# Moving one weight load ahead of a query load, and casts between VectorE and GpSimd, at the start of a fused attention and MLP kernel

## The chip, the cores and the metric

The kernel runs on one core of a Trainium2 chip. The metric is the time of one execution in microseconds (us) of device time. It is about 1.8 us longer than the span that the profile shows (first to last instruction). Engines are called as in the profile: PE is the matmul engine (TensorE), DVE is VectorE, ACT is ScalarE, POOL is GpSimd, SP issues DMAs. All timed runs of this study were in the fast state; the granted clock was 0.993 to 1.0 in all of them but three, which are named below. A load has landed when its data are in place.

## The reference, cut to what matters

```python
q_s = softmax(q, axis=-1)                    # q, k, v: (8 batches, 8 heads, 576, 64) f32
k_s = softmax(k, axis=2)                     # over the sequence
kv  = einsum('bhsd,bhse->bhde', k_s, v)      # 64 x 64 per head
x   = einsum('bhsd,bhde->bhse', q_s, kv)     # then laid out as (4608, 512)
h   = x @ w_in                               # 512 x 2048
g   = h * sigmoid(beta * h)
out = g @ w_out                              # 2048 x 512, f32
```

Inputs and outputs are float32; the kernel computes in bf16.

## The kernel before

Work runs in nine chunks of 512 rows of x (one per batch, and one for the leftover rows). For a chunk `c`, `mm_a(c, j)` computes one of 16 blocks of h (4 matmuls, then a tanh on ACT and a product on DVE, which gives `g`), and `mm_b(c, j)` adds `g` times a block of `w_out` into four accumulators (4 matmuls). In this text h_12 is `mm_a(0, 12)` of the first chunk, th_12 its tanh, g_12 its product. There are two PSUM buffers for h, so h_12 cannot start before tanh and product of h_10 are done.

While PE works on chunk 0, the weights still come in, and the attention of batch 1 is made ready: exp of q (ACT), row sum, reciprocal and multiply (DVE), transposes `tp` of q (PE) with an evacuation each (the copy out of PSUM, the memory that PE writes to), exp of k (ACT), cast of v to bf16, then `kv_mm` and `x_mm`.

```python
    load_q(0, parts=2); load_kv(k_st, k, 0, ...); load_kv(v_st, v, 0, ...)   # written in one line here
    ...
    w_load("in", 2)
    w_load("out", 2)
    load_q(1, parts=2)
    w_load("in", 3)                  # last block of w_in
    w_load("out", 3, 0)
    load_kv(k_st, k, 1, "k_st", parts=4)
    w_load("out", 3, 1)
    load_kv(v_st, v, 1, "v_st", parts=2)
    ...
    for kind, blk in (("in", 0), ("out", 0)):       # casts of the first weight blocks
        for half in range(2):
            if (kind, half) != ("in", 0):
                w_cast(kind, blk, half, nc.gpsimd)
    ...
    w_cast("in", 1, 0, nc.vector)
    mm_a(0, 2)
    mm_a(0, 3)
    w_cast("in", 1, 1, nc.vector)
    mm_b(0, 0)
    mm_b(0, 1)
    ...
    tail_zero(0)                                     # four memsets on POOL
    pool_cast(("out", 1), ("in", 2), ("out", 2))     # casts on POOL
    tail_zero(1)
    pool_cast(("in", 3), ("out", 3))

    for u in range(4, NJ):
        ...                                          # mm_a(0, u)
        if FIX and u in (12, 14):
            for j in (u - 12, u - 11):
                q_pet(1, j, nc.scalar if u == 12 else nc.vector)   # transposes
        mm_b(0, u - LAG)                             # LAG = 2
        if u in (9, 10):
            q_exp(1, u - 9)
        if u in (9, 11):
            q_sum(1, (u - 9) // 2)
        if u in (10, 12):
            q_mul(1, (u - 10) // 2)
        ...
        if u >= 12:
            kz_exp(1, u - 12)
        if u == 14:
            vz_cast(1, 0, nc.vector, m=2)
    mm_b(0, NJ - 2)
    vz_cast(1, 2, nc.vector, m=2)
    kv_mm(1, 0)
    kv_norm(1, 0)
    warm(2)                                          # two filler matmuls
    kv_mm(1, 1)
    kv_norm(1, 1)
    mm_b(0, NJ - 1)
    for j in range(HP):
        x_mm(1, j, ...)                              # first one: x_0 of batch 1
```

Each engine executes its instructions in the order of the program.

The softmax here doesn't subtract the row's maximum and nothing guards it: scores larger than these inputs give would overflow.

## Time and profile before

| | before |
|---|---|
| time, median of the first 3 runs | 290.23 us (290.08 to 290.25) |
| the profiled execution | 290.86 us, span 289.1 us |
| PE busy | 97% of the span, granted clock 1.0 |
| PE waits named after 51 us | only 0.2 us, in the last block |

From the page: the span, the busy times, and the slices of PE, its clock and the DMA engines.

```profile
span 289.1 us, 4130 instructions
...
PE 279.2 (97%) x1595; PEld 127.9 (44%) x1595; DVE 181.9 (63%) x281; ACT 163.7 (57%) x238; POOL 41.0 (14%) x55
...
PE   8899979999999999999999999999999999999994
...
PEclk9999999999999999999999999999999999999999
DMA  7999999907951982198129902794370033005003
```

PE is nearly always busy. One slice is 7.2 us; the DMA engines are full in slices 2 to 8, up to about 55 us, with the weights and the first batches. From there on PE sets the pace. The waits of PE say where the rest is:

```profile
PE h_12_520 L358 <- POOL w_in_b L145: 1.5, 1, 1.5
PE warm_153 L450 <- DVE kvp L478: 1.2, 1, 1.2
PE tp_0_200 L250 <- ACT ek_144 L158: 1.0, 1, 1.0
PE h_6_433 L358 <- DVE g_4_414 L370: 0.5, 1, 0.5
```

The second and third lie in the first 9 us and the change does not touch them. The PE timeline (columns: start, duration, engine, line, what, and in brackets the idle time before it and who ended it) gives the waits more exactly. A 512-column matmul starts 0.216 us after the one before it when nothing is in the way (the beat below), although its modelled duration is longer.

```profile
21.69 0.38 PE L386 MATMUL acc_3_380<-w_out_b,g_1_355 128*128 128x512 bf16 x1
22.16 1.04 PE L358 MATMUL h_4_407<-xT_80,w_in_b 128*128 128x512 bf16 x4
...
25.40 0.38 PE L386 MATMUL acc_3_380<-w_out_b,g_3_374 128*128 128x512 bf16 x1
26.30 1.02 PE L358 MATMUL h_6_433<-xT_80,w_in_b 128*128 128x512 bf16 x4 [0.51 <-DVE g_4_414 L370]
...
36.44 0.38 PE L386 MATMUL acc_3_380<-w_out_b,g_9_479 128*128 128x512 bf16 x1
38.34 0.60 PE L358 MATMUL h_12_520<-xT_80,w_in_b 128*128 128x512 bf16 x2 [1.52 <-POOL w_in_b L145]
...
49.95 0.38 PE L314 MATMUL x_0_666<-qsT_529,kvp 128*128 128x512 bf16 x1
```

Subtracting the beat: 0.25 us before h_4, 0.68 before h_6, 1.68 before h_12. The last line, x_0 of batch 1, is the mark by which I measure all versions below.

What held h_6 is on DVE and POOL. First DVE, then POOL:

```profile
21.40 0.69 DVE L145 CAST w_in_b<-w_in_102 128x1024 bf16<-128x1024 f32 x1 [0.96 <-DMA w_in_102<-in_moe_w_in_dram]
...
23.21 2.45 DVE L145 CAST w_in_b<-w_in_102 128x1024 bf16<-128x1024 f32 x1
25.57 0.67 DVE L370 SCALAR_TENSOR_TENSOR g_4_414<-th_4_412,h_4_407 128x512 bf16<-128x512 bf16 x1
```

```profile
22.63 1.04 POOL L145 CAST w_out_b<-w_out_100 128x1024 bf16<-128x1024 f32 x1 [4.53 <-DMA w_out_100<-in_moe_w_out_dram]
23.61 0.96 POOL L558 MEMSET vt_75<- 128x1040 bf16 x1
24.51 0.53 POOL L559 MEMSET ekt_77<- 128x512 bf16 x1
24.98 0.75 POOL L561 MEMSET vt_75<- 64x8 bf16 x2
...
36.65 2.62 POOL L145 CAST w_in_b<-w_in_114 128x1024 bf16<-128x1024 f32 x2 [2.11 <-DMA w_in_114<-in_moe_w_in_dram]
```

Two DVE casts of one shape took 0.69 and 2.45 us; the slow one ran beside POOL instructions. The Trainium skill, "SBUF — State Buffer", section "Who interferes with whom", explains it: DVE in a two-port mode and POOL take turns on a port pair, and the later one waits. The last POOL line is what held h_12: POOL had been idle for 2.11 us until the load of the last w_in block landed.

### The profile page before, as it was taken

Reading aid. Unit: us, or ns where it says so; the run is one execution under the profiler, and the core shown is the slowest. Engines: PE = TensorE matmul, PEld = TensorE weight load, DVE = VectorE, ACT = ScalarE, POOL = GpSimd, SP = SyncE. Lnnn points to the kernel's source line nnn. Section 1 sums busy time; section 2 is a strip of 40 time slices with the busy share of each in tenths; the row PEclk is TensorE's granted clock in tenths of the full one; section 3 lists DMA queues with packets and bytes.
Section 4 is the critical chain, followed back from the end, with each engine's and each line's share of the span. In section 5 each row is a group of like instructions: output and inputs, shape, how many; then the busy total and the mean of one; then the engine's idle time right before and its main releaser. Section 6 shows DMA issues by size and latency. Waiting matters only on the chain.

```text
span 289.1 us, 4130 instructions
## 1 busy us (share of the span) xinstructions
PE 279.2 (97%) x1595; PEld 127.9 (44%) x1595; DVE 181.9 (63%) x281; ACT 163.7 (57%) x238; POOL 41.0 (14%) x55
## 2 busy tenths in 40 slices
PE   8899979999999999999999999999999999999994
PEld 3443435444444444444444444444445444444441
DVE  7838577696569546945695469546954595454442
ACT  4762666694477356734683568355934563553341
POOL 4438660210030011000300030003000000000000
PEclk9999999999999999999999999999999999999999
DMA  7999999907951982198129902794370033005003
GB/s 228 383 384 364 379 389 315 285 2 183 322 168 40 309 218 95 50 322 225 64 84 234 313 29 120 171 259 116 145 213 7 1 147 73 0 0 147 0 0 145
DMA packets 56227, 50.08 MB, mean 173 GB/s; under 512 B 26240, under 2 KB 47760, under 8 KB 56208
## 3 DMA queue, kind: packets, MB, share of 16 engines
q1 hardware_dynamic: 56064, 49.56, 55.6%
q8 instruction: 12, 0.20, 0.3%
q10 hardware_dynamic: 144, 0.26, 0.2%
q14 instruction: 7, 0.06, 0.1%
HBM read 36.71 MB, written 9.44 MB: 160 GB/s over the span
## 4 chain that ended last, share of the span: by engine, by line
PE 83%; DMA 6%; DVE 5%; ACT 2%; SPq 1%; issue 1%; ACTq 0%
DMA w_in_102<-in_moe_w_in_dram 4%; DMA v_st_91<-in_v_dram 2%; PE acc_3_2822 L386 1%; PE acc_3_1636 L386 1%; PE acc_1_1026 L386 1%; PE acc_1_2820 L386 1%; PE acc_3_2577 L386 1%; PE acc_0_2248 L386 1%; PE acc_3_1940 L386 1%; PE acc_1_1938 L386 1%; PE acc_0_721 L386 1%; PE acc_1_2575 L386 1%; PE acc_0_2574 L386 1%; PE acc_2_2250 L386 1%; PE acc_1_1634 L386 1%; PE acc_3_1332 L386 1%
## 5 line engine op out<-in xcount | busy, mean ns | idle before, releaser
L358 PEld LDWEIGHTS <-w_in_b 128*128 128x128 bf16 x576 | 55.2, 98 | 70.5 <-issue 3.2
L145 POOL CAST va_2284<-v_st_2104 128x2048 bf16<-128x2048 f32 x1 | 1.9, 1919 | 30.7 <-DMA v_st_2104<-in_v_dram 30.7
L450 PEld LDWEIGHTS <-kvp 128*128 128x128 bf16 x34 | 3.6, 113 | 5.9 <-issue 3.1
L145 POOL CAST va_1669<-v_st_1489 128x2048 bf16<-128x2048 f32 x1 | 1.9, 1918 | 28.2 <-DMA v_st_1489<-in_v_dram 28.2
L145 POOL CAST va_1973<-v_st_1793 128x2048 bf16<-128x2048 f32 x1 | 1.9, 1916 | 25.9 <-DMA v_st_1793<-in_v_dram 25.9
L158 ACT ACTIVATE ek_144<-k_st_86 64x576 bf16<-64x576 f32 x8 | 5.4, 681 | 0.2
L158 ACT ACTIVATE ek_149<-k_st_118 64x576 bf16<-64x576 f32 x8 | 5.4, 677 | 0.0
L145 POOL CAST va_1061<-v_st_836 128x2048 bf16<-128x2048 f32 x1 | 1.9, 1918 | 24.2 <-DMA v_st_836<-in_v_dram 24.2
L314 PEld LDWEIGHTS <-kvp 128*128 128x128 bf16 x32 | 3.1, 98 | 4.3 <-DVE kvp L309 1.0
L145 POOL CAST va_1365<-v_st_1185 128x2048 bf16<-128x2048 f32 x1 | 1.9, 1919 | 21.4 <-DMA v_st_1185<-in_v_dram 21.4
L145 POOL CAST va_147<-v_st_91 128x576 bf16<-128x576 f32 x4 | 3.1, 805 | 6.5 <-DMA v_st_91<-in_v_dram 6.5
L214 ACT ACTIVATE eq_189<-q_st_83 128x1024 bf16<-128x1024 f32 x2 | 2.1, 1057 | 3.0 <-DMA q_st_83<-in_q_dram 3.0
L145 DVE CAST w_in_b<-w_in_102 128x1024 bf16<-128x1024 f32 x2 | 3.1, 1570 | 1.0 <-DMA w_in_102<-in_moe_w_in_dram 1.0
L145 POOL CAST va_783<-v_st_132 128x2048 bf16<-128x2048 f32 x1 | 1.9, 1919 | 12.4 <-DMA v_st_132<-in_v_dram 12.4
L145 POOL CAST w_in_b<-w_in_114 128x1024 bf16<-128x1024 f32 x2 | 2.6, 1334 | 2.1 <-DMA w_in_114<-in_moe_w_in_dram 2.1
L145 POOL CAST w_out_b<-w_out_100 128x1024 bf16<-128x1024 f32 x2 | 2.1, 1040 | 4.8 <-DMA w_out_100<-in_moe_w_out_dram 4.8
L225 DVE TENSOR_REDUCE rq_191<-eq_189 128x16 f32<-128x1024 bf16 x2 | 2.4, 1215 | 0.3 <-ACT eq_189 L214 0.3
L225 DVE TENSOR_REDUCE rq_487<-eq_485 128x16 f32<-128x1024 bf16 x2 | 2.4, 1216 | 0.3 <-ACT eq_485 L214 0.3
L225 DVE TENSOR_REDUCE rq_748<-eq_746 128x16 f32<-128x1024 bf16 x2 | 2.4, 1212 | 0.3 <-ACT eq_746 L214 0.3
L225 DVE TENSOR_REDUCE rq_1947<-eq_1945 128x16 f32<-128x1024 bf16 x2 | 2.4, 1192 | 0.3 <-ACT eq_1945 L214 0.3
L225 DVE TENSOR_REDUCE rq_2584<-eq_2582 128x16 f32<-128x1024 bf16 x2 | 2.4, 1191 | 0.3 <-ACT eq_2582 L214 0.3
L225 DVE TENSOR_REDUCE rq_1035<-eq_1033 128x16 f32<-128x1024 bf16 x2 | 2.4, 1191 | 0.3 <-ACT eq_1033 L214 0.3
(1448 smaller groups left out, 834.8 us busy)
## 6 DMA issues: line engine op xcount, KB each, us to landing
k_st_86<-in_k_dram SPq DMA_DIRECT2D x4, 288.0 KB, 5.9
v_st_91<-in_v_dram SPq DMA_DIRECT2D x4, 288.0 KB, 6.8
k_st_118<-in_k_dram SPq DMA_DIRECT2D x4, 288.0 KB, 9.6
v_st_124<-in_v_dram SPq DMA_DIRECT2D x2, 576.0 KB, 9.4
q_st_83<-in_q_dram SPq DMA_DIRECT2D x2, 512.0 KB, 4.3
w_in_97<-in_moe_w_in_dram SPq DMA_DIRECT2D x2, 512.0 KB, 6.4
w_out_100<-in_moe_w_out_dram SPq DMA_DIRECT2D x2, 512.0 KB, 9.4
w_in_102<-in_moe_w_in_dram SPq DMA_DIRECT2D x1, 1024.0 KB, 11.0
```

What stands on the lines that cost most here:

```text
L145: eng.tensor_copy(dst, src)
L158: nc.scalar.activation(ek[b][r, j : j + m, :, e * D : (e + 1) * D], k_st[b][r, j : j + m, :].rearrange("p j (i d) -> p j i d", i=RW), ACTF ...
L214: nc.scalar.activation(eq[b][:, :, s * m : (s + 1) * m, :].rearrange("p i h d -> p h i d"), q_st[b][:, s * m : (s + 1) * m, :].rearrange(" ...
L225: nc.vector.tensor_reduce(rq[b][:, 0, :, h], eq[b][:, :, h, :], axis=AX.X, op=ALU.add)
L314: nc.tensor.matmul(t[:], kvp[:, c, j, :], qsT[c][:, :, j, :])
L358: nc.tensor.matmul(h[:], w_in_b[:, kt, ds(j * P, P)], x_of(c)[:, kt, :], start=(kt == 0), stop=(kt == KT - 1),)
L386: nc.tensor.matmul(acc[st][:], g[:, ds(st * P, P)], w_out_b[:, j, :], start=(j == 0), stop=(j == NJ - 1),)
L450: nc.tensor.matmul(t[:, 0:cols], kvp[:, B - 1, 0, :], kvp[:, B - 1, :, :].rearrange("p j r -> p (j r)")[:, 0:cols],)
```

## The change

The intent is to take both waits away. The last w_in block is loaded in front of q of batch 1. One half cast of w_in block 1 goes from DVE to POOL. As q now comes later, its exp, sum and multiply stand one step later, and the transposes' evacuations all go to DVE; the v casts of batch 1 go to POOL. The last block's evacuations and stores are spread differently.

```diff
-            evac(eng, o[:, st, :], acc[st][:])
+            evac(nc.scalar if st in (0, 3) else nc.vector, o[:, st, :], acc[st][:])
...
-            (nc.sync, nc.scalar, nc.sync, nc.sync)[st].dma_start(ov[:, st, :], o[:, st, :])
+            (nc.scalar if st == R - 1 else nc.sync).dma_start(ov[:, st, :], o[:, st, :])
...
+    w_load("in", 3)
     load_q(1, parts=2)
-    w_load("in", 3)
...
-            if (kind, half) != ("in", 0):
+            if (kind, half) not in (("in", 0), ("out", 1)):
                 w_cast(kind, blk, half, nc.gpsimd)
...
     w_cast("in", 1, 0, nc.vector)
+    w_cast("in", 1, 1, nc.gpsimd)
+    w_cast("out", 0, 1, nc.gpsimd)
     mm_a(0, 2)
     mm_a(0, 3)
-    w_cast("in", 1, 1, nc.vector)
...
-        if FIX and u in (12, 14):
-            for j in (u - 12, u - 11):
-                q_pet(1, j, nc.scalar if u == 12 else nc.vector)
+        if u == 13:
+            for j in (0, 1):
+                q_pet(1, j, nc.vector)
         mm_b(0, u - LAG)
-        if u in (9, 10):  q_exp(1, u - 9)            # joined in one line here, as the five below
-        if u in (9, 11):  q_sum(1, (u - 9) // 2)
-        if u in (10, 12): q_mul(1, (u - 10) // 2)
+        if u in (10, 11): q_exp(1, u - 10)
+        if u in (10, 12): q_sum(1, (u - 10) // 2)
+        if u in (11, 13): q_mul(1, (u - 11) // 2)
...
-        if u == 14:
-            vz_cast(1, 0, nc.vector, m=2)
+    vz_cast(1, 0, nc.gpsimd, m=2)
+    vz_cast(1, 2, nc.gpsimd, m=2)
+    for j in (2, 3):
+        q_pet(1, j, nc.vector)
     mm_b(0, NJ - 2)
-    vz_cast(1, 2, nc.vector, m=2)
```

More of the change, by code (lines that the diff above doesn't have):

```diff
@@ L568 @@
     for u in range(4, NJ):
-        if not (FIX and u == 5):
+        if u != 5:
             mm_a(0, u)
-        if FIX and u == 4:
+        if u == 4:
             mm_a(0, 5)
@@ L574 @@
             continue
-        if FIX and u in (12, 14):
-            for j in (u - 12, u - 11):
-                q_pet(1, j, nc.scalar if u == 12 else nc.vector)
+        if u == 13:
+            for j in (0, 1):
+                q_pet(1, j, nc.vector)
         mm_b(0, u - LAG)
-        if u in (9, 10):
-            q_exp(1, u - 9)
-        if u in (9, 11):
-            q_sum(1, (u - 9) // 2)
+        if u in (10, 11):
+            q_exp(1, u - 10)
         if u in (10, 12):
-            q_mul(1, (u - 10) // 2)
-        if not FIX and u in (11, 13):
-            for j in (u - 11, u - 10):
-                q_pet(1, j, nc.scalar if u == 11 else nc.vector)
+            q_sum(1, (u - 10) // 2)
+        if u in (11, 13):
+            q_mul(1, (u - 11) // 2)
         if u >= 12:
             kz_exp(1, u - 12)
-        if u == 14:
-            vz_cast(1, 0, nc.vector, m=2)
+    vz_cast(1, 0, nc.gpsimd, m=2)
+    vz_cast(1, 2, nc.gpsimd, m=2)
+    for j in (2, 3):
+        q_pet(1, j, nc.vector)
     mm_b(0, NJ - 2)
-    vz_cast(1, 2, nc.vector, m=2)
     kv_mm(1, 0)
```

## The prediction

> What bounds the kernel now. The page gives PE 97% of a 289.1 us span at clock 1.0; PE's waits list nothing from 51 us to the last block, so only the first 51 us and the tail can yield. In PE's timeline, against its 0.216 us beat per 512-column matmul:
> - 0.68 us before h_6 (25.62 to 26.30). The chain goes through the second half cast of w_in block 1 on DVE: 2.45 us, its twin 0.69. POOL ran a cast and memsets then. The Trainium skill, "SBUF — State Buffer", section "Who interferes with whom", says a DVE copy in a two-port mode and a GpSimd instruction take one port pair in turn, the later blocking fully; this trace agrees. g_4 queued behind it.
> - 1.69 us before h_12 (36.65 to 38.34): the last w_in block lands at 36.5, its POOL half cast took 1.63.
> - 0.2 to 0.3 us each around kv_mm of batch 1 and the x evacuations (47 to 51 us).
>
> What moves. The first loads run at about 380 GB/s without a hole from 5 to 46 us and land in order: w_out block 2 at 30.8, q halves of batch 1 at 32.3 and 33.8, w_in block 3 at 36.5, v halves of batch 1 at 43.8 and 45.3. After the swap w_in 3 lands near 33.6, q halves near 35.0 and 36.5, v as before.
> - h_6: the half cast goes to POOL (1.04 us). Both halves start on one landing (21.4) and contend; with DVE first, w_out 0's second half ends near 24.1 and costs its matmul (due at 23.9) about 0.25 us. POOL first would cost h_4 1 us. Gain 0.4 to 0.7.
> - h_12: both casts end near 36.5, the first before h_12 is due (36.0). The 1.69 us goes away.
> - Given back: ScalarE executes in order, and q_exp of the first half, now after th_10, waits for q until 35.0; so th_11, the row sum (1.22+0.25) and g_11 come late (38.2). h_13, due at 37.7, needs h_11's buffer: 0.5 us. The first transposes need q_mul (1.21): 0.25 us.
> - kv_mm of batch 1: v casts on POOL (estimate 1.2 us each, from 0.66 us per 576 columns) follow the landings: 43.8 to 45.0, 45.3 to 46.5. The first kv_mm also waits for the DVE evacuations of tp_2 and tp_3: about 45.7. The second waits for the v cast and the last k exp (1.36 us per pair, ScalarE full from 38.5 to 46.0): about 46.7, against 48.51 before. This, not PE, is the new limit.
> So x_mm of batch 1 starts near 48.2 instead of 49.95: gain 1.75 us. Later work is PE-bound and shifts as a block.
> - Tail: the last evacuation goes from DVE (0.69) to ScalarE (0.59), its store issued from there, but closer behind the store before it (0.4 us instead of 0.64): 0 to 0.1 us.
>
> Predicted: 290.23 - 1.75 - 0.05 = about 288.5; allowing for waits not seen, 288.6. Range 288.0 to 289.6. Faster by over 2% would need 5.8 us, more than all PE idle time beside start and tail: 1%. Slower by over 2%: 1%.
>
> What would show it. POOL's wait before h_12 and DVE's before h_6 gone; a ScalarE wait for q near 34 to 36 us, new PE waits of some tenths before h_13 and tp_0; the second kv_mm of batch 1 released by the POOL cast or k exp near 46.7; x_0 of batch 1 near 48.2; the span after it as before, within 0.1 us.
>
> What would make it wrong. POOL first at 21.4 us; q landing later than 36.5, which feeds exp, sum, multiply and transposes; v casts on POOL blocked by DVE; ScalarE's store landing later. Each is under 1 us. More gain than 2.2 us would need v to land earlier.

## The result

The change took 289.07 us (median of 6 runs, 288.60 to 290.53); the kernel before, beside it, 290.14 (6 runs, 289.75 to 290.25). The ratio is 0.997, with a 95% interval of 0.9948 to 0.9992. A ratio here is the mean time of one kernel's runs over that of the other's of the same rounds, so it is not quite the ratio of the medians. The change is faster by about 1.1 us, which is within 2%, as predicted, and inside the predicted range; but the gain is two thirds of the 1.63 us forecast (290.23 - 288.6).

The page after:

```profile
span 286.8 us, 4132 instructions
...
PE 277.9 (97%) x1595; PEld 127.7 (45%) x1595; DVE 180.0 (63%) x280; ACT 162.9 (57%) x236; POOL 43.7 (15%) x58
...
PE   7799999999999999999999999999999999999994
```

The spans of the two profiled executions differ by 2.3 us, more than twice the difference of the medians. So the pair of traces cannot simply be subtracted, and the first thing to find out is why. The PE timeline after, at the same places (in this trace the names have no numbers; by position the lines are h_6, then h_12, the four matmuls of mm_b(0, 10), h_13, the first two transposes of batch 1, and x_0 to x_3 of batch 1):

```profile
25.29 1.03 PE L358 MATMUL h<-xT,w_in_b 128*128 128x512 bf16 x4
...
35.65 1.03 PE L358 MATMUL h<-xT,w_in_b 128*128 128x512 bf16 x4
36.51 1.03 PE L386 MATMUL acc<-w_out_b,g 128*128 128x512 bf16 x4
37.37 1.03 PE L358 MATMUL h<-xT,w_in_b 128*128 128x512 bf16 x4
39.02 0.61 PE L250 MATMUL tp<-identity,eq 128*128 128x128 bf16 x8 [0.62 <-ACT ek L158]
...
47.70 1.03 PE L314 MATMUL x<-qsT,kvp 128*128 128x512 bf16 x4
```

The waits before h_6 and h_12 are gone. A new one of 0.79 us (1.65 us from start to start, less four beats of 0.216) stands before the transposes. The view names an exp of k on ACT as what ended it, but transposes of q do not read k; the q multiply on DVE ended 0.14 us before they started, and it is what they read. DVE and POOL there:

```profile
36.95 1.93 DVE L231 TENSOR_TENSOR eq<-eq,rq 128x1024 bf16<-128x1024 bf16 x1
```

```profile
33.38 2.02 POOL L145 CAST w_in_b<-w_in 128x1024 bf16<-128x1024 f32 x2
36.76 1.04 POOL L145 CAST w_out_b<-w_out 128x1024 bf16<-128x1024 f32 x1 [1.36 <-DMA w_out<-in_moe_w_out_dram]
```

The multiply, 1.21 us in the trace of before, took 1.93. A POOL cast had started 0.19 us ahead of it. The skill's section quoted above says that a DVE instruction with two SBUF inputs contends with a POOL instruction that reads SBUF, and the experiment wout_dve tests it. The first POOL line shows the two casts of w_in block 3 in 2.02 us, with no wait in front: the load had landed at 32.36 us, as the swap intends.

### The profile page after: what moved, and what is told of

It is laid out like the page before. It is cut to its first block, busy times and chain, and to the rows that moved or that the text cites. A ratio compares the mean times of both kernels' runs of the same rounds, so it can differ in the third digit from the quotient of the medians.

```text
span 286.8 us, 4132 instructions
## 1 busy us (share of the span) xinstructions
PE 277.9 (97%) x1595; PEld 127.7 (45%) x1595; DVE 180.0 (63%) x280; ACT 162.9 (57%) x236; POOL 43.7 (15%) x58
## 4 chain that ended last, share of the span: by engine, by line
PE 84%; DMA 11%; SPq 1%; POOL 1%; ACT 1%; issue 0%; DVE 0%; ACTq 0%
PE acc L386 40%; PE h L358 39%; DMA w_in<-in_moe_w_in_dram 6%; DMA k_st<-in_k_dram 5%; PE x L314 2%; PE kv L276 2%; POOL w_in_b L145 1%; PE kv L264 0%; PE tp L250 0%; SPq L85 0%; SPq L106 0%; PE x L318 0%; ACT ek L158 0%; DVE g L370 0%; ACT th L368 0%
## 5 line engine op out<-in xcount | busy, mean ns | idle before, releaser
L368 ACT ACTIVATE th<-h,beta_t 128x512 bf16<-128x512 f32 x144 | 98.5, 687 | 102.6 <-PE h L358 100.7
L370 DVE SCALAR_TENSOR_TENSOR g<-th,h 128x512 bf16<-128x512 bf16 x144 | 97.9, 682 | 92.2 <-ACT th L368 90.7
L358 PE MATMUL h<-xT,w_in_b 128*128 128x512 bf16 x576 | 146.1, 379 | 0.5 <-ACT xT L143 0.2
L386 PE MATMUL acc<-w_out_b,g 128*128 128x512 bf16 x576 | 145.9, 379 | 0.2 <-DVE g L370 0.2
L386 PEld LDWEIGHTS <-g 128*128 128x128 bf16 x576 | 56.0, 98 | 67.9 <-DVE g L370 1.0
L145 POOL CAST va<-v_st 128x2048 bf16<-128x2048 f32 (+2 forms) x12 | 17.3, 1460 | 145.0 <-DMA v_st<-in_v_dram 145.0
L225 DVE TENSOR_REDUCE rq<-eq 128x16 f32<-128x1024 bf16 x18 | 21.6, 1198 | 2.3 <-ACT eq L214 2.3
L231 DVE TENSOR_TENSOR eq<-eq,rq 128x1024 bf16<-128x1024 bf16 x18 | 22.6, 1257 | 0.1
L214 ACT ACTIVATE eq<-q_st 128x1024 bf16<-128x1024 f32 x16 | 16.3, 1048 | 2.9 <-DMA q_st<-in_q_dram 2.9
L169 ACT ACTIVATE ek<-k_st 128x1024 bf16<-128x1024 f32 x12 | 12.6, 1047 | 0.0
```

Source lines behind the costliest of these rows:

```text
L145: eng.tensor_copy(dst, src)
L169: nc.scalar.activation(ek[b][:, :, h, :].rearrange("p i h d -> p h i d"), k_st[b][:, h, 0 : R * D].rearrange("p h (i d) -> p h i d", i=R), ...
L214: nc.scalar.activation(eq[b][:, :, s * m : (s + 1) * m, :].rearrange("p i h d -> p h i d"), q_st[b][:, s * m : (s + 1) * m, :].rearrange(" ...
L225: nc.vector.tensor_reduce(rq[b][:, 0, :, h], eq[b][:, :, h, :], axis=AX.X, op=ALU.add)
L231: nc.vector.tensor_tensor(eq[b][:, :, h, :], eq[b][:, :, h, :], rq[b][:, 1, :, h].unsqueeze(3).to_broadcast((P, R, m, D)), ALU.mult,)
L358: nc.tensor.matmul(h[:], w_in_b[:, kt, ds(j * P, P)], x_of(c)[:, kt, :], start=(kt == 0), stop=(kt == KT - 1),)
```

## The experiments

All were timed over five rounds beside the kernel before, in three groups, each on a chip of its own: c_before, c_after, undo_load, undo_wcast; then wout_dve, tp_later, undo_vcast, undo_tail; then c_after2, only_load, q_halves, q_halves_nowarm. Only the first and the third hold a repeat of the change, so a time of the second group has none beside it. To compare the traces I list for each when the load of w_in block 1 landed (all versions issue the same loads up to there), when the first half of q of batch 1 landed, when x_0 of batch 1 started, how long after that landing, and the span. They are worked out from the landing records and the PE timelines.

```
                 w_in 1 landed   q landed   x_0 started   x_0 after q   span
before               21.38         32.32       49.95          17.63       289.1
c_before             19.63         31.31       49.01          17.70       288.2
the change           19.63         33.87       47.70          13.83       286.8
c_after              19.55         34.39       48.23          13.84       287.4
c_after2             19.74         34.26       48.10          13.84       287.2
undo_load            21.80         32.60       49.35          16.75       288.5
only_load            19.87         34.26       50.14          15.88       289.3
undo_wcast           19.44         34.33       48.16          13.83       287.3
wout_dve             19.64         33.96       47.48          13.52       286.6
tp_later             19.55         34.47       47.98          13.51       287.1
undo_vcast           19.80         34.34       49.18          14.84       288.3
undo_tail            19.81         34.19       48.03          13.84       287.2
q_halves             19.76         31.65       47.76          16.11       286.9
q_halves_nowarm      20.02         32.30       47.95          15.65       287.1
```

In every one of these traces the time from x_0 to the last matmul's start is 234.57 to 234.60 us, and from there to the end of the span 4.52 to 4.57 us. So whatever a version does, it does before x_0 of batch 1.

### c_before, c_after, c_after2: both kernels again

No edit.

> The kernel before, unchanged, for a second trace of it. Theory L (landings): in the trace of before, the w_in block 1 load landed at 21.4 us, in that of the change at 19.6, although both issue the same loads up to there; a 16 KB instruction fetch that sits in one DMA engine for 1.1 us near 19 us falls in different places, and every later landing is late by about 1.1 us in one and not in the other. Then this trace may show either landing (19.6 or 21.4), w_in block 3 lands at 35.3 or 36.5, and the wait before h_12 is 0.5 to 1.7 us accordingly. Rival P (program): the late landing belongs to the kernel before. Then w_in block 1 lands at 21.4 again and the time is within 0.3 us of the medians so far. Ratio to before 0.999 to 1.001 under both.

> The changed kernel, unchanged. Its six runs spread over 1.9 us (288.6 to 290.53), the six of before over 0.5. Theory L: landings after 20 us are 0 to 1.2 us later than in the first trace; if late, q halves land at 35.0 and 36.5, k at 38.6 and v at 43.8 and 45.3, and PE waits 0.5 us before h_13 and up to 1 us before tp_0. Rival C (collision): the spread comes from the q multiply on DVE meeting the POOL cast of w_out block 3 (1.93 us in the first trace against 1.21 alone); then landings agree with the first trace within 0.3 us and only that wait changes. Ratio to before 0.994 to 0.999.

> The changed kernel once more, beside the last three. x_0 of batch 1 starts at 47.7 to 48.3 us, PE waits 0.8 to 1.1 us before the first transposes, ratio to before 0.995 to 0.998.

Measured: c_before 290.07 us, ratio 0.9998 (0.9976 to 1.0019); c_after 289.21, 0.9963 (0.9943 to 0.9982); c_after2 288.94, 0.9954 (0.9940 to 0.9968). So the gain of the change is confirmed at 1.0 to 1.3 us.

In c_before the load of w_in block 1 landed at 19.63 us, as in the trace of the change: the kernel before does not always have the late landing. It is late in 2 of the 14 traces, before and undo_load. Both have the old load order, which has three traces; but the loads whose order differs are issued only at 21.87 us or later, when w_in block 1 has landed in every trace, so the order itself can hardly be the reason. Two traces are too few to say more. The PE timeline of c_before (h_6, h_12 and x_0 of batch 1):

```profile
25.36 1.02 PE L358 MATMUL h<-xT,w_in_b 128*128 128x512 bf16 x4
...
37.40 0.39 PE L358 MATMUL h<-xT,w_in_b 128*128 128x512 bf16 x1 [1.52 <-POOL w_in_b L145]
...
49.01 1.03 PE L314 MATMUL x<-qsT,kvp 128*128 128x512 bf16 x4
```

The waits before h_4 and h_6, 0.93 us in the first trace, are 0.09 here. The difference of 0.84 us, and 0.08 from the first loads, is what x_0 starts earlier by (0.94). The wait before h_12 is 1.68 us in both. The times suggest that c_before is the usual case and that the profile I predicted from had caught one of the slower executions: of 45 timed executions of that kernel, two were as long as its 290.86 us, one of them at a granted clock of 0.993.

And yet the slow DVE cast is there in c_before as well, 2.65 us beside the same POOL instructions:

```profile
22.07 2.65 DVE L145 CAST w_in_b<-w_in 128x1024 bf16<-128x1024 f32 x1
```

```profile
21.69 1.04 POOL L145 CAST w_out_b<-w_out 128x1024 bf16<-128x1024 f32 x1 [3.68 <-DMA w_out<-in_moe_w_out_dram]
```

The DVE cast starts at 22.07 us against 23.21 in the first trace, is done at 24.72, and the products behind it are in time for h_6. A cast can be slow without costing anything.

With the early landing on both sides, the gain can be accounted for. Each number is a sum of waits in the PE timeline (time from start to start, less the beat):

```
                                   c_before   change   c_after   c_after2
before h_4 and h_6                   0.09      0        0         0
before h_12                          1.68      0        0         0
before h_13                          0         0        0.32      0
before the first transposes          0         0.79     1.08      1.09
before both kv_mm of batch 1         0.49      0.16     0.16      0.16
sum                                  2.26      0.95     1.56      1.25
start of h in full (all four k)     17.94     17.95    17.87     18.04
x_0 of batch 1                      49.01     47.70    48.23     48.10
```

The sums and the starts differ as x_0 does, to 0.02 us: 2.26 - 1.56 + 0.07 = 0.77 for c_after, against 49.01 - 48.23 = 0.78. Of the 2.10 us that the change removes (0.09 + 1.68 + 0.33), 0.8 to 1.4 us is given back before h_13 and the transposes. Between c_after and the first trace of the change, q landed 0.5 us later (34.39 and 35.88 us instead of 33.87 and 35.35): this is theory L on a smaller scale, and the multiply took 1.93 us in both, so rival C does not explain the spread between these two. The one run of 290.53 us has no trace and stays unexplained.

The table at the head of this section shows more. In the three traces of the change, and in undo_wcast and undo_tail, x_0 starts 13.83 or 13.84 us after the first half of q has landed, although that landing moves by 0.52 us; the first transposes start 5.15 to 5.17 us after it. So in the changed kernel the landing of q sets the place of x_0, and a wait of PE that is removed ahead of the transposes is only waited for again there. Counted from that landing, the traces can be compared without the scatter of the loads.

### undo_load: the old load order in the change

```diff
-    w_load("in", 3)
     load_q(1, parts=2)
+    w_load("in", 3)
```

> The change with the old load order (q of batch 1 in front of the last w_in block). If the swap carries the gain in full, h_12 waits 1.7 us again and the time is 1.7 us above the change. If, as I think, part of that time is given back anyway because the second kv_mm of batch 1 waits for v and its cast, it is 0.6 to 1.1 us above the change. If the swap only trades one wait for another (head of line wait for q on ScalarE), the same as the change within 0.2 us.

Measured: 289.62 us, ratio 0.9976 (0.9955 to 0.9997), 0.4 us above c_after of the same rounds. This is less than I expected and the intervals overlap. The profiled execution again waits before h_12 (1.35 us), but not before the transposes; it had the late landing, so it is no fair measure of the size. The direction agrees with a partial give-back: the swap in the changed kernel trades 1.4 to 1.7 us before h_12 for 0.8 to 1.4 us before h_13 and the transposes.

### only_load: the load swap alone in the kernel before

```diff
+    w_load("in", 3)
     load_q(1, parts=2)
-    w_load("in", 3)
```

> The kernel before with the load swap alone. Theory H (head of line): q_exp of the first half stands on ScalarE behind th_9 and waits there from 32.2 us until q lands near 34, so th_10, the row sum and g_10 come 1.5 us late and h_12, which needs h_10's buffer, starts near 37.1, hardly earlier than the 37.4 of before: time within 0.3 us of before. Rival: w_in's landing is the only thing that holds h_12; then h_12 starts near 35.7 and the time falls by 1 us or more.

Measured: 291.64 us, ratio 1.0054 (1.0029 to 1.0079): slower than before, and not within 0.3 us of it. The median overstates the loss: three of the six runs had a granted clock of 0.991, the lowest, and took 292.11 to 293.40 us; why is not known. The other three, at 0.998 to 1.0, took 290.94 to 291.17, about 1 us above the 290.16 of before, and x_0 in the trace (clock 0.998) starts 1.13 us later than in c_before. My mechanism held, my size did not. ACT, with th_9, the first exp of q, and th_10:

```profile
31.94 0.69 ACT L368 ACTIVATE th<-h,beta_t 128x512 bf16<-128x512 f32 x1 [1.04 <-remote]
34.28 1.06 ACT L214 ACTIVATE eq<-q_st 128x1024 bf16<-128x1024 f32 x1 [1.65 <-DMA q_st<-in_q_dram]
35.24 0.67 ACT L368 ACTIVATE th<-h,beta_t 128x512 bf16<-128x512 f32 x1
```

The exp waits for q with th_10 standing behind it, and PE gets h_12 at 37.47 us although the last cast of its weights had ended at 35.8:

```profile
37.47 1.02 PE L358 MATMUL h<-xT,w_in_b 128*128 128x512 bf16 x4 [1.25 <-DVE g L370]
39.42 0.61 PE L250 MATMUL tp<-identity,eq 128*128 128x128 bf16 x8 [0.93 <-DVE eq L231]
```

I expected that much (37.1). On top of it the later multiplies, of 1.94 and 1.89 us, each meet a POOL cast, and the two pairs of transposes wait 1.09 and 0.47 us. The load order and the place of the exp have to move together; the load order alone is a loss.

### undo_wcast: the half cast of w_in block 1 back on DVE

```diff
-            if (kind, half) not in (("in", 0), ("out", 1)):
+            if (kind, half) != ("in", 0):
...
-    w_cast("in", 1, 1, nc.gpsimd)
-    w_cast("out", 0, 1, nc.gpsimd)
     mm_a(0, 2)
     mm_a(0, 3)
+    w_cast("in", 1, 1, nc.vector)
```

> The change with the second half cast of w_in block 1 back on DVE in its old place. The 0.7 us wait before h_6 comes back with a DVE cast of about 2.4 us. If PE sets the pace up to 45 us, the time is 0.6 to 0.7 us above the change. If the q multiply and the landings set it (PE waited 0.8 us before tp_0 anyway), at most 0.2 us above.

Measured: 288.85 us, ratio 0.9955 (0.9935 to 0.9974), not slower than c_after. No wait came back before h_6, and not even the slow cast did. DVE and POOL:

```profile
21.90 0.68 DVE L145 CAST w_in_b<-w_in 128x1024 bf16<-128x1024 f32 x1
```

```profile
22.01 1.48 POOL L145 CAST w_out_b<-w_out 128x1024 bf16<-128x1024 f32 x1 [4.17 <-DMA w_out<-in_moe_w_out_dram]
```

Here DVE came first by 0.11 us and kept its 0.68; POOL paid, 1.48 instead of 1.04. In c_before POOL came first (its cast from 21.69, DVE's from 22.07) and DVE took 2.65. The skill's section says the order of issue decides who blocks; these two traces show it, and the order hangs on when a load lands. PE did wait 0.16 us before mm_b(0, 2) and 0.13 us before mm_b(0, 4), whose weights POOL cast a little later; but x_0 again starts 13.83 us after q landed, so these waits cost nothing in the end. Moving this cast gained nothing that these runs can see.

### wout_dve: one w_out half cast on DVE behind the multiply

```diff
-    pool_cast(("in", 3), ("out", 3))
+    pool_cast(("in", 3))
...
         if u in (11, 13):
             q_mul(1, (u - 11) // 2)
+            w_cast("out", 3, (u - 11) // 2, nc.vector if u == 11 else nc.gpsimd)
```

> The change with the first half cast of w_out block 3 on DVE behind the first q multiply, instead of on POOL. In both traces of the change PE waits 0.8 to 1.1 us before the first transposes of batch 1, behind a q multiply of 1.93 us that starts just after that POOL cast; alone it takes 1.21. Theory P (shared port): the multiply takes 1.2 us, the wait falls by 0.7 us to 0.1 to 0.4, and the time by 0.5 to 0.7 us against the change. Theory Q (late q): the wait comes from the late landing of q and the multiply's length does not matter; the wait stays within 0.2 us and so does the time.

Measured: 288.64 us, ratio 0.9956 (0.9943 to 0.9969). DVE (the multiply), then PE (first and second pair of transposes):

```profile
37.05 1.21 DVE L231 TENSOR_TENSOR eq<-eq,rq 128x1024 bf16<-128x1024 bf16 x1
```

```profile
38.40 0.61 PE L250 MATMUL tp<-identity,eq 128*128 128x128 bf16 x8
...
43.50 0.61 PE L250 MATMUL tp<-identity,eq 128*128 128x128 bf16 x8
```

With no POOL cast beside it the multiply takes 1.21 us again, and the wait before the transposes falls from 0.79 to 0.19 us with q landing within 0.1 us of the first trace of the change. Theory P is confirmed for the wait. These transposes started at 38.40, while the first pair of k exps ran until 39.03; so the name that the view gave for their wait in the change was wrong. But x_0 moved only from 47.70 to 47.48, because 0.31 us came back before the second pair of transposes. Counted from the landing of q, x_0 is 0.32 us earlier than in the change (13.52 us against 13.84). In time it is 0.74 us below undo_tail of the same rounds, but only 0.3 to 0.6 us below the repeats of the change in other rounds: a gain, of a size that stays rough.

### tp_later: the first transposes behind mm_b(0, 11)

```diff
-        if u == 13:
-            for j in (0, 1):
-                q_pet(1, j, nc.vector)
         mm_b(0, u - LAG)
+        if u == 13:
+            for j in (0, 1):
+                q_pet(1, j, nc.vector)
```

> The change with the first two transposes behind the four matmuls of mm_b(0, 11) instead of in front. PE then has 0.86 us of work while the q multiply runs. If the wait before the transposes is what the change gives back, it disappears (at most 0.2 us left) and the time falls by 0.6 to 0.9 us against the change. If v's landing and cast are the limit, as predicted, the second kv_mm of batch 1 waits for POOL instead and the time falls by less than 0.3 us.

Measured: 288.89 us, ratio 0.9956 (0.9945 to 0.9968); 0.5 us below undo_tail of the same rounds, and no different from c_after2 in others. In the trace, with landings within 0.1 us of c_after's, x_0 starts 0.25 us earlier (47.98 against 48.23), and 0.33 us earlier counted from the landing of q. Both expectations missed: the wait did not vanish into filler, and POOL was not what came next. PE waits 0.39 us before h_13, and then 0.22, 0.24 and 0.17 us before the transposes, h_15 and the second transposes. DVE is busy without a break from 35.58 to 45.7 us: the whole row of sums, multiplies, products and evacuations hangs on the landing of q and runs at DVE's pace.

### undo_vcast: the v casts back on DVE

```diff
-    vz_cast(1, 0, nc.gpsimd, m=2)
-    vz_cast(1, 2, nc.gpsimd, m=2)
     for j in (2, 3):
         q_pet(1, j, nc.vector)
+    vz_cast(1, 0, nc.vector, m=2)
     mm_b(0, NJ - 2)
+    vz_cast(1, 2, nc.vector, m=2)
```

> The change with the v casts of batch 1 back on DVE (0.75 us each), the first in front of mm_b(0, 14), the second behind it. They queue behind the evacuations of the transposes, which end near 45.4 us; the second cast then ends near 47, so the second kv_mm waits 0.3 to 0.6 us more than in the change: time 0.3 to 0.6 us above the change. If the move to POOL brought nothing, within 0.15 us.

Measured: 289.92 us, ratio 0.9995 (0.9983 to 1.0007): the whole gain of the change is gone. DVE, then PE (first `kv_mm` of batch 1):

```profile
45.16 0.75 DVE L145 COPY qsT<-tp 128x512 bf16<-128x512 bf16 x2
45.83 1.42 DVE L145 CAST va<-v_st 128x1152 bf16<-128x1152 f32 x2
```

```profile
46.73 0.74 PE L264 MATMUL kv<-va,ek 128*128 128x65 bf16 x18 [1.00 <-DVE va L145]
```

In the trace the loss is 1.00 us (x_0 at 14.84 us after q landed, against 13.84); in time it is 0.5 us above undo_tail of the same rounds and 0.7 to 1.0 above the repeats of the change in others. In the trace it is larger than I expected, because both casts queue behind the evacuations and the first kv_mm, not only the second, has to wait: 1.16 us instead of 0.16. With all four evacuations on DVE, moving the v casts to POOL is what makes the new order pay.

### undo_tail: the last block as before

```diff
-            evac(nc.scalar if st in (0, 3) else nc.vector, o[:, st, :], acc[st][:])
+            evac(eng, o[:, st, :], acc[st][:])
...
-            (nc.scalar if st == R - 1 else nc.sync).dma_start(ov[:, st, :], o[:, st, :])
+            (nc.sync, nc.scalar, nc.sync, nc.sync)[st].dma_start(ov[:, st, :], o[:, st, :])
```

> The change with the last block's evacuations and stores as before. From the last matmul's start to the end of the span the trace of before shows 4.56 us; theory: the change's tail is 0 to 0.1 us shorter, so this one is 0 to 0.1 us above the change, which the timing cannot resolve; the trace's tail decides.

Measured: 289.38 us, ratio 0.9976 (0.9964 to 0.9988). The trace's tail, last matmul's start to the end, is 4.57 us; in the versions with the new tail it is 4.52 to 4.56. So the tail is worth 0 to 0.05 us. The times stand 0.2 to 0.4 us above the change's in other rounds, which the trace does not explain (x_0 at 48.03, the tail as said); it shows how far differences of this size can be read across rounds.

### q_halves: q split around the last w_in block

```diff
+    load_q(1, parts=2, only=0)       # first half; load_q takes only=... for it
     w_load("in", 3)
-    load_q(1, parts=2)
+    load_q(1, parts=2, only=1)
...
-        if u in (10, 11): q_exp(1, u - 10)
-        if u in (10, 12): q_sum(1, (u - 10) // 2)
+        if u in (9, 11): q_exp(1, (u - 9) // 2)
+        if u in (9, 12): q_sum(1, (u - 9) // 3)
```

> An improvement: the change with the first q half loaded in front of the last w_in block and the second behind it, and the first exp and row sum moved up from u = 10 to 9, the second row sum unchanged. The chain of exp, sum and multiply on ScalarE and DVE then starts near 33 us instead of 35. If that chain is what holds the change back, the waits before h_13 and both pairs of transposes vanish (0.2 us in sum at most), the second kv_mm waits for nothing or for the v cast, and the time falls by 0.6 to 0.9 us against the change. If v's landing is the limit, as predicted, less than 0.2.

Measured: 288.37 us, ratio 0.9936 (0.9922 to 0.9950), the fastest version: 0.57 us below c_after2 of the same rounds. All six runs (288.27 to 288.77) lie near or below the fastest of c_after2 (288.70), though the intervals of the ratios overlap a little. PE (first transposes, first kv_mm of batch 1), then DVE:

```profile
38.35 0.61 PE L250 MATMUL tp<-identity,eq 128*128 128x128 bf16 x8
...
45.31 0.74 PE L264 MATMUL kv<-va,ek 128*128 128x65 bf16 x18 [0.66 <-DVE qsT L145]
```

```profile
44.14 0.69 DVE L370 SCALAR_TENSOR_TENSOR g<-th,h 128x512 bf16<-128x512 bf16 x1 [0.86 <-ACT th L368]
44.74 0.75 DVE L145 COPY qsT<-tp 128x512 bf16<-128x512 bf16 x2
```

The waits before h_12, h_13 and both pairs of transposes are gone, with the q halves landing at 31.65 and 35.88 us and w_in between them at 34.39. A new one of 0.82 us stands before the first kv_mm: its PSUM buffer is held by a transpose whose evacuation stands on DVE behind g_15, and g_15 waits for th_15, which stands on ACT among the exps of k. PE would reach this kv_mm at 44.5 us, about 0.6 us before that evacuation was done. It still is not the v cast: the second kv_mm follows the filler without a wait.

### q_halves_nowarm: the same without the filler

```diff
     kv_norm(1, 0)
-    warm(2)
```

> The same without the two filler matmuls (0.43 us) in front of the second kv_mm of batch 1. With the q chain out of the way that kv_mm would start near 45.1 and v's POOL cast ends near 45.4 to 45.9, so the filler hides a wait: 0 to 0.2 us below q_halves. If PE sets the pace, 0.4 us.

Measured: 288.65 us, ratio 0.9941 (0.9927 to 0.9956), no faster than q_halves. The loads of this profiled execution ran 0.6 us later, so its trace says little of the filler by itself. Within the resolution of these runs the filler costs nothing.

## Why the prediction was right or wrong

The time fell into the range, and the place of x_0 was close: predicted near 48.2 us, found at 47.70, 48.23 and 48.10. That x_0 came so close is in part luck: the prediction had the first half of q landing at 35.0 us and x_0 13.2 us later, held by v; q landed at 33.87 to 34.39 us and x_0 came 13.84 us later, held by the q work, and the two errors nearly cancelled. The gain was over-stated, and two steps of the prediction failed: the base that it was subtracted from (1) and the limit that it named (4). The other points are terms that held or were mis-sized.

1. **The base.** The step "Predicted: 290.23 - 1.75". The 1.75 us came from a trace whose execution took 290.86 us and was subtracted from a median that is 0.63 us lower. That trace contains the waits before h_4 and h_6 of 0.93 us, of which I counted "0.4 to 0.7" as gain; c_before has 0.09 there, undo_wcast shows that the moved cast buys nothing, and what differs ahead of these waits is the landing of w_in block 1, 1.75 us later in the first trace than in c_before. Had I added up the predicted end from x_0 at 48.2 us (234.58 to the last matmul, 4.56 to the end of the span, 1.76 to the time), I would have said 289.1, which is what was measured.
2. **h_12.** "The 1.69 us goes away": it does, in every trace of the change, and it is 1.68 us in c_before too.
3. **Given back.** Predicted 0.5 us before h_13 and 0.25 before the transposes, 0.75 together; measured 0.79, 1.40 and 1.09 in three traces. The late q was part of it, as said. Mis-sized was the term "q_mul (1.21)": it took 1.93 in each of them, held by a POOL cast of w_out that lands just then. The 0.5 us before h_13 was seen once, with 0.32.
4. **The new limit.** The step "This, not PE, is the new limit", meaning v's landing and its POOL cast, failed. The second kv_mm follows the filler with no wait in all three traces of the change (in the first, at 46.26 us, with the last v cast done at 45.35). What holds the change is the row of q work on ACT and DVE, fed by the landing of q (x_0 13.83 or 13.84 us after it in five traces): moving its first half up (q_halves) took those waits away, and the next one in line was a PSUM buffer behind the same engine.
5. **POOL's casts of v.** The pair took 2.71 us, predicted 2.4; it was off PE's path. That they had to leave DVE was not in the prediction as a gain, and it is worth 1.0 us in the trace, 0.5 to 1.0 in the times.
6. **The port race at 21.4 us.** POOL did come first in the change (19.69 us, DVE's cast at 20.29 took 0.99 instead of 0.69), but the loads landed while DVE still had products to do, and nothing was lost.
7. **The tail.** Predicted 0 to 0.1 us; the traces show 0 to 0.05.

What stays open: why a load lands early or late, which in the changed kernel sets the time. In each of the 14 traces a packet of 16 KB in an instruction queue occupies a DMA engine for 1.05 to 1.13 us from about 19 us on, when the loads in question are under way. In the two late traces the first load to land after it, w_in block 1, is late by 1.7 us; in the other twelve that load is in time and those behind it are late by 0.5 to 1.25 us (8.29 and 8.31 us from the first half of w_out block 0 to w_out block 1 in the late ones, 7.27 to 8.02 in the others, against an estimate of 6.8 from the 2.7 us per MB of the loads around). That is association; no experiment moved the packet.

## What to carry to other kernels

Before subtracting waits read in one trace from a median of other runs, compare the time of the profiled execution with that median, and take a second trace: a wait that hangs on when a load lands may be in one and not in the next. When a load is moved back, walk the whole in-order queue of every engine that reads it: the exp, sum, multiply and evacuation behind it inherit the delay, and the load swap without the matching move of the exp was a loss of about 1 us. And put DVE instructions with two SBUF inputs, or casts between SBUF tiles, where no GpSimd cast starts just before them, above all if PE waits for the result.

## What the Trainium skill lacked or had wrong

- "SBUF — State Buffer", section "Who interferes with whom": it says that the later of two instructions blocks until the first finishes. In c_before a DVE cast that found POOL in a cast (to end at 22.73 us) ran from 22.07 to 24.72 us, through two memsets of POOL behind that cast as well; alone it takes 0.69. It looks as if a row of POOL instructions can keep the pair over several of them (two traces, no experiment); the page names only the one under way.
- The same section, on two SBUF inputs against a POOL read: confirmed, and with a size here. The multiply took 1.21 us alone and 1.93 to 1.94 when a POOL cast of 1.04 us had started 0.17 to 0.19 us ahead of it. The 0.72 us more are the rest of that cast (0.85) less 0.13.
- "Runtime: NRT & Kernel Launch", section "Instruction fetch mechanics": it calls the cost of crossing a 16 KiB block of instructions "mostly hidden". Neither it nor another page gives the time that a fetch may take from the kernel's loads. Here such a packet held an engine for 1.05 to 1.13 us in every trace, and the landings behind it came 0.5 to 1.7 us later than the rate of the loads around would have them (the link is argued, not shown).
- No page tells how much the landing of one and the same load varies from run to run: w_in block 1 landed between 19.44 and 21.80 us in 14 traces.
